# Packed attention with a gated FFN, one core: the first batch's loads, TensorE's first products and the first f tiles in another order

## The chip, the cores and the metric

One core of one Trainium2 chip runs the whole program. The metric is the device time of one execution in microseconds (us). The kernel before takes 739.77 us (median of 3 runs, 739.72 to 740.54).

## The reference

For each of 8 batches and 8 heads, 32 packed queries p attend over 576 keys and values, and the 576 queries q then attend over the 32 packed results. The output x, one row per token, goes through a gated feed-forward layer.

```python
def sm_attn(qq, kk, vv):                     # scale = 1 / sqrt(64)
    s = scale * np.matmul(qq, kk.transpose(0, 1, 3, 2))
    ...                                      # softmax a of s over the last axis
    return np.matmul(a, vv)
p_packed = sm_attn(p, k, v)                  # p: 8 x 8 x 32 x 64; q, k, v: 8 x 8 x 576 x 64
out = sm_attn(q, p_packed, p_packed)
x = out.transpose(0, 2, 1, 3).reshape(4608, 512)
return (x @ w_a) * (x @ w_b) @ w_out         # w_a, w_b: 512 x 1536; w_out: 1536 x 512
```

## The kernel before, in words

The work runs batch by batch; all of it is one stream on TensorE, with the other engines feeding it. For a batch:

- **Stage 1** (`stage1`, L241 on): scores of p against k (products at L247), softmax (maximum L253, exponential L257, both over two groups of heads e = 0, 1), its transposition (L271, L272) and the product with v (L281). The result pp is turned into `ppT` (L236, L237).
- **Stage 2** (`stage2`, L289 on): scores of q against pp (L297), a 32 x 32 transposition on VectorE (L302), maximum (L304), subtraction (L307), exponential (L309), sum and reciprocal (L312 to L314), multiplication (L315), transposition back (L318). The weights of the softmax are split in a high part `a_hi` (L319, ScalarE) and a low part `a_lo` (L86, VectorE) for TensorE's faster number format.
- **g tiles** (`g_tiles`, L324 on): the product of pp with the columns of w_a and w_b for a pair of f tiles (L332, 64x512 moving), split the same way into `ghi` (L338) and `glo` (L86). Since x = a2 @ pp, x @ w is computed as a2 @ (pp @ w).
- **First layer** (`mm1`, L355 on): for each of the 12 f tiles, 12 products of `ghi`, `glo` with `a_hi`, `a_lo` for the w_a half and 12 for the w_b half (L351); ScalarE copies one half (L363), VectorE multiplies (L366), the product is split into h_hi (L370) and h_lo (L86 on GpSimd).
- **Second layer** (`mm2_part`, L377): h times w_out into the output tiles.

The weights are read once, in pieces of 512 KB (`load_w`, `load_wout`), each as two 32-bit halves of what is stored. A piece takes three steps: A, `high_word` on ScalarE (L189); B, `low_word` on ScalarE, VectorE or GpSimd, as a digit of the string `WAYS` says (0: L197, 1 and 2: L194); C, `both_words` on VectorE (L200), which writes the piece into `w_ab`. A pool of 12 buffers holds pieces between load and C. Four pieces fill one pair of f tiles (index c).

The order on every engine is written out by hand. `FIRST` is the order of the first loads, `START` of everything up to the first product of `mm1`, `PLAN_0` and `PLAN` of what is put between the steps of `mm1` and `mm2` (slot by slot), as tokens: `T0` turns p, `k0` to `k4` and `q0` to `q4` turn pieces of k and q (`turn_first`, L147, L152, copies L149, L154, on the engine that the string `TURN` says), `S` and `r` step stage 1, `s` steps stage 2, `P0` turns pp, A, B, C convert a weight piece, `g` is the first pair of g tiles, and `W` puts nine products into TensorE's stream (`warm`, L524) whose result nobody reads. All loads of the first batch are issued from one queue, SyncE's (SP). A queue waits before a load until the load eight places before it, in the order in which the program issues them, has landed.

Of the kernel before, what the change touches and what calls it, by code (L numbers as in the profile page):

```python
# [9 lines left out]
F32R = mybir.dt.float32r  # L10
# [9 lines left out]
def tile_packed_attn_gated_ffn(  # L20
# [105 lines left out]
    def load_first(src, key, part):  # L126

        if part < 2:
            t = scratch.tile([P, R, 4 * D], F32, name=f"{key}n{part}")
            nc.sync.dma_start(  # L130
                out=t, in_=src[0, R * part:R * part + R, 0:4 * P, :].rearrange("h (p i) d -> p h (i d)", i=4))
        else:
            t = scratch.tile([P, H, 2 * D], F32, name=f"{key}n{part}")
            nc.sync.dma_start(out=t[0:TR], in_=src[0, :, 4 * P:S, :].rearrange("h (p u) d -> p h (u d)", u=2))
        firsts[key, part] = t
# [22 lines left out]
    def load_v(b, e):  # L158
# [5 lines left out]
        for i in range(4 // n):  # L164
            nc.sync.dma_start(
                out=t[:, :, n * i:n * i + n, :].rearrange("p r u d -> p r (u d)"),
                in_=vv[n * P * i:n * P * i + n * P].rearrange("(p u) r d -> p r u d", u=n).rearrange("p r u d -> p r (u d)"))
        for u in range(2):
            nc.sync.dma_start(
                out=t[TR * u:TR * u + TR, :, 4, :],  # L170
                in_=vv[4 * P:S].rearrange("(p u) r d -> u p r d", u=2)[u])
        vts[b, e] = t

    def load_p(b):
        t = sm.tile([P, E + 1, D], F32, name="p_nat", bufs=1)
        for e in range(E + 1):
            nc.sync.dma_start(out=t[:, e, :], in_=p[b].rearrange("(r e) j d -> e r j d", e=E)[e % E])  # L177
        p_nat[b] = t
# [27 lines left out]
    def load_w(c, n):  # L206

        w, rr = (w_a, w_b)[n // 2], n % 2
# [211 lines left out]
    def emit(b, plan, tasks={}):  # L420

        for name in plan.split():
# [3 lines left out]
            if name == "W":  # L426
                warm()
                continue
# [27 lines left out]
            elif what == "Lp":  # L456
# [4 lines left out]
    FIRST = ("p0 k0 k2 k1 q0 v0 q1 v1 q2 w1 w1 w1 w1 w1 w1 w1 w1 w1 w1 w1")  # L461
    START = ("T0 k0 k4 k1 k3 k2 q0 S0 S1 r0 r1 q1 r1 r0 r0 r1 r0 q2 r1 q3 q4 P0 s0 B s1 W A s0 B A A s0 s0 B s1 C "
             "A s1 B s0 C s1 A s1 C B B Lp2 C A B A s0 s1 B C B B s0 B g A C A A s1 Lv2 Lk2 C C A A C B B Lk3 C s1")
    WAYS = ("000000022220202120012012011200010010")
    TURN = ("0001110101")
    SUBS = ("0100")
# [4 lines left out]
    PLAN_0 = ("A | C C | B A B A | B C C B C | A A | C | B | C B A T0 k0 Lp2 A | A A B B C Lq0 | C C k1 | A B A | "  # L471
# [18 lines left out]
    def convert(x):  # L490
# [16 lines left out]
        else:  # L507
            assert len(to_do["A"]) <= len(to_do[x]) and len(to_do["B"]) <= len(to_do[x])
            if c < NC:
# [23 lines left out]
    for name in FIRST.split():  # L533
        what, i = name[0], int(name[1])
        if what == "p":
            load_p(0)
        elif what == "v":
            load_v(0, i)
        elif what == "w":
            load_pieces(i)  # L540
        else:
            load_first(k if what == "k" else q, what, i)
    gnext = []
    tasks = {"g": next_g(0)}
    emit(0, START, tasks)
    drain(tasks["g"])
    early.__exit__(None, None, None)
# [5 lines left out]
    for b in range(B):  # L553
        plan = dict(PLAN if b else PLAN_0)
        slot, tasks = [0], {"g": next_g(b + 1)}
# [5 lines left out]
        for ft in range(NFT):  # L561
            if ft % 2 == 0:
                gcur = list(gnext)
            elif ft + 1 < NFT:
# [64 lines left out]
```

## Time and profile before

| | |
|---|---|
| median of 3 runs | 739.77 us |
| the profiled execution, its own time | 739.7 us |
| its span (first to last instruction) | 737.9 us |
| outside the span | 1.8 us |
| TensorE busy | 724.8 us, 98% of the span |
| VectorE, ScalarE, GpSimd busy | 302.4, 282.6 and 212.5 us |
| data moved | 58.3 MB |

Times in the trace are microseconds from the span's start. TensorE has two records for one product, its weight load (PEld) and the product (PE); a product of two 4-byte operands is two instructions on it. "Idle before" is what an engine waited ahead of a row, with the instruction or load that ended the wait. The row of the granted clock in the page stands at full speed throughout; at which of its two levels TensorE ran is seen in the length of equal instructions.

### The profile page before, as it was taken

The numbers are of one execution on the slowest core, as the hardware profiler recorded it, in microseconds if no ns is written. First come the engines' busy times: TensorE is split into PE (matmuls) and PEld (weight loads), VectorE is DVE, ScalarE is ACT, GpSimd is POOL, SyncE is SP. The second block draws the span as 40 slices with busy tenths as digits, with TensorE's granted clock in tenths as the row PEclk, the third lists the DMA queues.
The fourth block names the chain that finished last, engine by engine and source line by source line (L and its number), as shares of the span: only waits on it lengthen the run. The fifth ranks groups of instructions, "written<-read, shape, count | busy, mean of one in ns | idle before, by whom it ended". The sixth has DMA issues, their size and how long they took to land.

```text
span 737.9 us, 13756 instructions
## 1 busy us (share of the span) xinstructions
PE 724.8 (98%) x5862; PEld 606.0 (82%) x5862; DVE 302.4 (41%) x487; ACT 282.6 (38%) x495; POOL 212.5 (29%) x154
## 2 busy tenths in 40 slices
PE   6899999999999999999999999999999999999998
PEld 4488977888888888888888888888888888888887
DVE  2888655456114561344503545045610456023200
ACT  3788744553125531444204442144311543134300
POOL 0586752334003340234202341033400334023300
PEclk9999999999999999999999999999999999999999
DMA  8999945250501514033310333115050100000001
GB/s 251 379 260 297 257 88 99 57 97 17 97 30 33 98 30 84 16 66 70 74 48 16 65 71 77 47 33 97 5 104 30 34 1 17 28 15 2 1 29 43
DMA packets 171005, 58.30 MB, mean 79 GB/s; under 512 B 140608, under 2 KB 158784, under 8 KB 170944
## 3 DMA queue, kind: packets, MB, share of 16 engines
q1 hardware_dynamic: 170944, 57.43, 31.9%
q8 instruction: 46, 0.75, 0.4%
q14 instruction: 15, 0.12, 0.1%
HBM read 47.97 MB, written 9.44 MB: 78 GB/s over the span
## 4 chain that ended last, share of the span: by engine, by line
PE 95%; DVE 2%; DMA 1%; ACT 1%; issue 0%; SPq 0%; DVEq 0%; ACTq 0%
PE m L351 42%; PE m L377 40%; PE x L332 6%; PE s L281 2%; PE s L247 1%; PE s L271 1%; PE s L297 1%; DMA raw<-in_moe_w_b_dram 1%; DMA kn<-in_k_dram 1%; PE x L236 0%; DVE w_ab L200 0%; PE x L147 0%; PE m L297 0%; PE m L147 0%; SPq L177 0%
## 5 line engine op out<-in xcount | busy, mean ns | idle before, releaser
L377 PE MATMUL m<-wo,h_hi 128*128 128x512 f32 (+1 forms) x888 | 268.7, 385 | 0.0
L86 POOL TENSOR_TENSOR h_lo<-asb,h_hi 128x576 fp32r<-128x576 f32 x96 | 139.1, 1449 | 411.5 <-ACT h_hi L370 411.2
L377 PEld LDWEIGHTS m<-wo,h_hi 128*128 128x128 f32 x888 | 164.2, 188 | 39.0 <-DVE t L302 5.0
L366 DVE TENSOR_TENSOR asb<-m,asb 128x576 f32<-128x576 f32 x96 | 72.7, 757 | 281.9 <-PE m L351 278.6
L351 PE MATMUL m<-a_hi,ghi 128*128 128x288 f32 x768 | 170.7, 304 | 1.6 <-ACT ghi L338 1.5
L377 PE MATMUL m<-wo,h_lo 128*128 128x512 f32 (+1 forms) x444 | 170.4, 384 | 0.0
L351 PE MATMUL m<-a_lo,ghi 128*128 128x288 f32 x768 | 164.0, 295 | 0.3 <-DVE a_lo L86 0.3
L351 PEld LDWEIGHTS m<-a_hi,ghi 128*128 128x128 f32 x768 | 122.2, 188 | 37.5 <-issue 15.9
L351 PE MATMUL m<-a_hi,glo 128*128 128x288 f32 x768 | 133.5, 295 | 0.0
L351 PEld LDWEIGHTS m<-a_lo,ghi 128*128 128x128 f32 x768 | 123.5, 188 | 0.5 <-DVE a_lo L86 0.5
L370 ACT CAST h_hi<-asb 128x576 fp32r<-128x576 f32 x96 | 64.7, 674 | 143.6 <-DVE asb L366 143.5
L351 PEld LDWEIGHTS m<-a_hi,glo 128*128 128x128 f32 x768 | 112.8, 188 | 0.2 <-DVE glo L86 0.2
L377 PEld LDWEIGHTS m<-wo,h_lo 128*128 128x128 f32 x444 | 83.4, 188 | 16.6
L86 DVE TENSOR_TENSOR glo<-x,ghi 128x512 fp32r<-128x512 f32 x96 | 61.8, 686 | 53.3 <-ACT ghi L338 53.3
L363 ACT COPY asb<-m 128x576 f32<-128x576 f32 x96 | 61.6, 641 | 36.7 <-PE m L351 29.0
L412 ACT COPY asb<-m 128x512 f32<-128x512 f32 x24 | 14.1, 587 | 134.8 <-PE m L377 133.6
L332 PE MATMUL x<-w_ab,ppT 64*32 64x512 f32 x768 | 55.4, 597 | 0.2 <-DVE w_ab L200 0.2
L338 ACT CAST ghi<-x 128x512 fp32r<-128x512 f32 x96 | 51.4, 588 | 5.9 <-PE x L332 5.9
L119 DVE STREAM_TRANSPOSE xT<-nat 128x1152 f32<-128x1152 f32 x28 | 38.3, 1368 | 0.0
L412 ACT COPY wo_f<-m 128x512 f32<-128x512 f32 x11 | 6.5, 588 | 55.2 <-PE m L377 55.2
L315 POOL TENSOR_TENSOR t<-t,sum 128x576 f32<-128x576 f32 x14 | 16.5, 1178 | 25.0 <-DVE sum L314 25.0
L189 ACT ACTIVATE raw<-raw 128x512 f32<-128x512 f32 x36 | 23.1, 683 | 0.1
(108 smaller groups left out, 408.1 us busy)
## 6 DMA issues: line engine op xcount, KB each, us to landing
nat<-in_k_dram SPq DMA_DIRECT2D x56, 144.0 KB
nat<-in_q_dram SPq DMA_DIRECT2D x56, 144.0 KB
vt<-in_v_dram SPq DMA_DIRECT2D x28, 256.0 KB
raw<-in_moe_w_a_dram SPq DMA_DIRECT2D x12, 512.0 KB
raw<-in_moe_w_b_dram SPq DMA_DIRECT2D x12, 512.0 KB
raw<-in_moe_w_out_dram SPq DMA_DIRECT2D x12, 512.0 KB
out_dram<-asb SPq DMA_DIRECT2D x17, 256.0 KB
out_dram<-wo_f SPq DMA_DIRECT2D x10, 256.0 KB
```

The costliest lines, as they stand in the source:

```text
L86: return eng.tensor_tensor(out=dst, in0=src, in1=hi.bitcast(F32), op=ALU.subtract)
L119: nc.vector.transpose(out=xT.rearrange("p h t -> p (h t)"), in_=t.rearrange("p h x d -> p (h x d)"))
L189: nc.scalar.activation(out=high, in_=high, func=AF.Prelu, scale=2.0 ** -112, alpha=-2.0 ** 32)
L315: eng.tensor_tensor(out=s2, in0=s2, in1=sum2.unsqueeze(2).broadcast_to([P, TU, J]), op=ALU.mult)
L332: nc.tensor.matmul(out=gps[e][J * r:J * r + J, :], lhsT=ppT[rows, 2 * (b % 2), r, :], rhs=w_ab[rows, c, r, :], start=True, stop=True)
L338: nc.scalar.copy(out=ghi[:, e], in_=gps[e])
L351: nc.tensor.matmul(out=ps[:, half, 0:HS], lhsT=gt[:, kt, i, :], rhs=at[:, kt, HS * half:HS * half + HS], start=(n == 0 and kt == 0), stop= ...
L363: nc.scalar.copy(out=asb, in_=pa[:, :, 0:HS])
L366: nc.vector.tensor_tensor(out=asb, in0=pb[:, :, 0:HS], in1=asb, op=ALU.mult)
L370: nc.scalar.copy(out=hh, in_=flat)
L377: nc.tensor.matmul(out=o[:, cols], lhsT=ht[:, c0:c0 + P], rhs=wt[:, cols], start=(ft == 0 and n == 0), stop=(ft == NFT - 1 and n == 2))
L412: nc.scalar.copy(out=ob, in_=o)
```

## The change

What it does:

- The loads of the first batch: k comes first, on SP's queue, then the first q tiles and the second v tile; p, the first v tile and the last piece of q are issued from ScalarE's queue (a capital letter in `FIRST`).
- `V13`: thirteen products of the 128x128 identity with itself stand at the head of TensorE's order, ahead of k; `W` becomes `W12`, twelve products instead of nine. Neither result is read.
- The first pair of f tiles is split: its weight pieces hold one f tile of w_a or w_b each, and `first_g` computes the g tiles of one f tile at a time, from two pieces (tokens `g` and `h`), with eight products of 256 columns for each.
- `TURN` moves four of the ten copies of turned k and q between VectorE and ScalarE, `SUBS` gives both subtractions and multiplications of stage 2 to GpSimd, `WAYS` moves the low words of some pieces, and `START` and `PLAN_0` are rewritten.

```diff
-    FIRST = ("p0 k0 k2 k1 q0 v0 q1 v1 q2 w1 w1 w1 w1 w1 w1 w1 w1 w1 w1 w1")
...
-    WAYS = ("000000022220202120012012011200010010")
-    TURN = ("0001110101")
-    SUBS = ("0100")
+    FIRST = ("k0 k1 k2 q0 P0 q1 V0 v1 w1 w1 w1 w1 w1 Q2 w1 w1 w1 w1 w1 w1")
+    START = ("V13 k1 T0 k3 k4 k0 k2 q0 S0 S1 r0 r1 q1 r1 r0 r0 r1 r0 B q2 r1 q3 A q4 P0 B C s0 s1 A A B W12 B s0 "
...
+    WAYS = ("100002012202202020012012011200010010")
+    TURN = ("1001000101")
+    SUBS = ("0000")
...
     def load_w(c, n):
+        if c == 0:
+            raw = wop.tile([P, R, P, 2], U32, name="raw", tag="w")
+            nc.sync.dma_start(
+                out=raw.rearrange("p r f t -> p r (f t)"),
+                in_=(w_a, w_b)[n % 2].bitcast(U32)[:, 2 * P * (n // 2):2 * P * (n // 2) + 2 * P].rearrange(
+                    "(r p) f -> p r f", p=P))
+            raws[c, n] = raw
+            return
...
-    def warm(n=9):
-        x = bank_pair()[:, 0, :]
-        t = firsts["k", 0].rearrange("p h t -> p (h t)")
+    def warm(t, n):
+        x = bank_pair()[:, 0, 0:t.shape[1]]
         for _ in range(n):
-            nc.tensor.matmul(out=x, lhsT=ident, rhs=t[:, 0:512], start=True, stop=True)
+            nc.tensor.matmul(out=x, lhsT=ident, rhs=t, start=True, stop=True)
+
+    def first_g(u, tiles):
...
+        gps = [bank() for _ in range(E)]
+        for r in range(R):
+            for e in range(E):
+                rows = slice(64 * e, 64 * e + 64)
+                nc.tensor.matmul(
+                    out=gps[e][J * r:J * r + J, 0:2 * P], lhsT=ppT[rows, 0, r, :],
+                    rhs=w_ab[rows, 0, r, :].rearrange("p (a u f) -> p u a f", a=2, u=2)[:, u],
+                    start=True, stop=True)
...
+        for e in range(E):
+            src = gps[e][:, 0:2 * P].rearrange("p (a f) -> p a f", a=2)
+            nc.scalar.copy(out=hi[:, e], in_=src)
+            lo_part(lo[:, e], src, hi[:, e])
...
+    tasks = {"g": first_g(0, firsts_g), "h": first_g(1, firsts_g)}
```

TensorE's order from its first instruction to the first scores of stage 1 (kn0, kn1, kn2 and qn0 are loaded pieces of k and q, p_nat is p). Before:

```order
L236 MATMUL x<-ident,p_nat 128x128 x2
L147 MATMUL x<-ident,kn_101 128x128 x4
L152 MATMUL x<-ident,kn_103 128x32 x8
L147 MATMUL x<-ident,kn_101 128x128 x4
L147 MATMUL m<-ident,kn_105 128x128 x8
L147 MATMUL x<-ident,qn_107 128x128 x4
L247 MATMUL s<-xT_147,pT 32x288 x2
```

And with the change:

```order
L535 MATMUL m<-ident 128x128 x13
L147 MATMUL x<-ident,kn_97 128x128 x4
L244 MATMUL x<-ident,p_nat 128x128 x2
L147 MATMUL m<-ident,kn_99 128x128 x4
L152 MATMUL x<-ident,kn_101 128x32 x8
L147 MATMUL x<-ident,kn_97 128x128 x4
L147 MATMUL m<-ident,kn_99 128x128 x4
L147 MATMUL x<-ident,qn_103 128x128 x4
L255 MATMUL s<-xT_157,pT 32x288 x2
```

The thirteen products stand in front, p behind the first piece of k, and the second half of k (kn_99) is wanted before the small last piece (kn_101).

TensorE's order from the second group of stage 2's scores to the first products of `mm1`. Before, and then with the change:

```order
L297 MATMUL m<-xT_185,ppT 32x288 x4
L524 MATMUL m<-kn_101,ident 128x512 x9
L332 MATMUL x<-w_ab,ppT 32x512 x8
L351 MATMUL m<-a_hi,ghi 128x288 x2
```

```order
L305 MATMUL m<-xT_199,ppT 32x288 x4
L535 MATMUL m<-kn_97,ident 128x512 x12
L544 MATMUL x<-w_ab,ppT 32x256 x16
L359 MATMUL m<-a_hi,ghi 128x288 x2
```

Twelve products instead of nine stand between the scores and the g tiles, and the g tiles of both f tiles (eight products each, sixteen in the row) still stand ahead of the first product of `mm1`.

The head of the two load queues. Before, all on SP's:

```order
L177 DMA p_nat<-in_p_dram 128x1x64 x3
L130 DMA kn_101<-in_k_dram 128x4x256
L134 DMA kn_103<-in_k_dram 32x8x128
L130 DMA kn_105<-in_k_dram 128x4x256
L130 DMA qn_107<-in_q_dram 128x4x256
L165 DMA vt<-in_v_dram 128x4x256
L169 DMA vt<-in_v_dram 32x4x64 x2
L130 DMA qn_113<-in_q_dram 128x4x256
```

With the change, SP's and then ScalarE's:

```order
L130 DMA kn_97<-in_k_dram 128x4x256
L130 DMA kn_99<-in_k_dram 128x4x256
L134 DMA kn_101<-in_k_dram 32x8x128
L130 DMA qn_103<-in_q_dram 128x4x256
L130 DMA qn_109<-in_q_dram 128x4x256
```

```order
L177 DMA p_nat<-in_p_dram 128x1x64 x3
L165 DMA vt<-in_v_dram 128x4x256
L169 DMA vt<-in_v_dram 32x4x64 x2
L134 DMA qn_129<-in_q_dram 32x8x128
L149 ACT_TABLE_LOAD
L149 COPY xT_158<-m 128x2x256
L149 COPY xT_157<-x 128x2x256
```

k goes to the head of SP's queue; p, the first v tile and the end of q are issued by ScalarE ahead of its first own instruction.

## Rows read from the trace of the kernel before

**Rows 1.** The page: TensorE's line of the busy times, and of the 40 slices of the span TensorE's busy tenths and the DMA engines'.

```profile
PE 724.8 (98%) x5862; PEld 606.0 (82%) x5862; DVE 302.4 (41%) x487; ACT 282.6 (38%) x495; POOL 212.5 (29%) x154
...
PE   6899999999999999999999999999999999999998
...
DMA  8999945250501514033310333115050100000001
```

**Rows 2.** What TensorE waited for in the whole span: engine, its line, what released it: us in total, times, longest.

```profile
PE x L236 <- DMA p_nat<-in_p_dram: 4.2, 1, 4.2
PE x L147 <- DMA kn<-in_k_dram: 2.2, 1, 2.2
PE m L351 <- ACT ghi L338: 1.5, 1, 1.5
...
PE m L351 <- DVE a_lo L86: 0.3, 1, 0.3
```

**Rows 3.** TensorE's timeline from 23 to 41 us, single rows of it.

```profile
23.90 7.99 PE L524 MATMUL m<-kn,ident 128*128 128x512 f32 x18
32.04 1.57 PE L332 MATMUL x<-w_ab,ppT 64*32 64x512 f32 x16 [0.15 <-DVE w_ab L200]
35.09 0.54 PE L351 MATMUL m<-a_hi,ghi 128*128 128x288 f32 x2 [1.48 <-ACT ghi L338]
...
37.68 0.53 PE L351 MATMUL m<-a_lo,ghi 128*128 128x288 f32 x2 [0.27 <-DVE a_lo L86]
...
39.20 1.22 PE L332 MATMUL x<-w_ab,ppT 64*32 64x512 f32 x16
```

**Rows 4.** The timeline of SP's queue from 0 to 19 us, in order of time: start, length of the issue (not of the transfer), what is loaded.

```profile
0.74 1.96 SPq L177 DMA_DIRECT2D p_nat<-in_p_dram  x3
2.74 0.48 SPq L130 DMA_DIRECT2D kn<-in_k_dram  x1
...
12.32 0.38 SPq L210 DMA_DIRECT2D raw<-in_moe_w_a_dram  x1
...
18.29 0.89 SPq L210 DMA_DIRECT2D raw<-in_moe_w_a_dram  x1
```

**Rows 5.** The DMA engines from 0 to 25 us, in 40 slices of 0.625 us: busy tenths, and GB/s moved.

```profile
DMA  0000227799999999999999999999999999999999
GB/s 0 0 0 23 46 47 98 184 349 370 271 295 341 351 354 347 352 332 276 295 342 351 353 304 215 239 305 390 387 383 393 380 390 397 374 383 393 387 374 400
```

**Rows 6.** TensorE's timeline from 7 to 21 us: start, length, what it does.

```profile
7.29 1.11 PE L147 MATMUL x<-ident,kn 128*128 128x128 f32 x4 [2.17 <-DMA kn<-in_k_dram]
8.33 1.06 PE L152 MATMUL x<-ident,kn 32*128 32x32 f32 x8
...
10.23 1.91 PE L147 MATMUL m<-ident,kn 128*128 128x128 f32 x8
11.93 1.06 PE L147 MATMUL x<-ident,qn 128*128 128x128 f32 x4
12.92 1.00 PE L247 MATMUL s<-xT,pT 64*32 64x288 f32 x24
13.74 0.90 PE L247 MATMUL m<-xT,pT 64*32 64x288 f32 x24
...
18.42 0.66 PE L147 MATMUL m<-ident,qn 128*128 128x128 f32 x4
...
20.43 0.68 PE L152 MATMUL x<-ident,qn 32*128 32x32 f32 x8
```

**Rows 7.** Timeline of VectorE, ScalarE and GpSimd from 24 to 36 us, single rows of the way from the scores of stage 2 to `a_hi` and `ghi`.

```profile
24.55 1.16 POOL L307 TENSOR_TENSOR s<-s,mx 128x576 f32<-128x576 f32 x1 [23.25 <-DVE mx L304]
...
25.74 0.69 ACT L309 ACTIVATE s<-s 128x576 f32<-128x576 f32 x1 [1.26 <-POOL s L307]
25.86 0.69 DVE L200 SCALAR_TENSOR_TENSOR w_ab<-raw 128x512 uint32<-128x512 uint32 x1
...
27.14 0.73 DVE L312 TENSOR_REDUCE sum<-s 128x18 f32<-128x576 f32 x1
...
28.54 1.41 POOL L315 TENSOR_TENSOR s<-s,sum 128x576 f32<-128x576 f32 x1 [2.83 <-DVE sum L314]
...
30.31 0.98 DVE L315 TENSOR_TENSOR s<-s,sum 128x576 f32<-128x576 f32 x1
...
32.42 1.43 DVE L318 STREAM_TRANSPOSE a2f<-s 128x576 f32<-128x576 f32 x2
33.22 1.33 ACT L319 CAST a_hi<-a2f 128x576 fp32r<-128x576 f32 x2 [1.15 <-DVE a2f L318]
```

**Rows 8.** Timeline of VectorE and the others from 1 to 22 us (ScalarE's table load, GpSimd's last step on the identity, a copy of turned k, the first maximum, pp, ppT).

```profile
0.73 1.28 ACT L154 ACT_TABLE_LOAD   x1 [0.73 <-PEq L613]
...
1.01 0.29 POOL masks.py:199 TENSOR_SCALAR_AFFINE_SELECT ident<-ident 128x128 f32<-128x128 f32 x1
...
12.18 0.69 DVE L149 COPY xT<-m 128x512 f32<-128x512 f32 x1 [1.01 <-PE m L147]
...
14.12 0.76 DVE L253 TENSOR_REDUCE nmx<-s 128x1 f32<-128x576 f32 x1 [1.25 <-PE s L247]
...
18.56 0.48 DVE L287 TENSOR_SCALAR pp<-x,rs 128x64 f32<-128x64 f32 x2 [1.08 <-PE x L281]
```

**Rows 9.** What SP's queue waited for between 17.3 and 18.8 us.

```profile
SPq L210 <- DMA raw<-in_moe_w_a_dram: 0.4, 1, 0.4
```

More of the change, by code (lines that the diff above doesn't have):

```diff
@@ L164, in load_v @@
         for i in range(4 // n):
-            nc.sync.dma_start(
+            eng.dma_start(
                 out=t[:, :, n * i:n * i + n, :].rearrange("p r u d -> p r (u d)"),
@@ L168, in load_v @@
         for u in range(2):
-            nc.sync.dma_start(
+            eng.dma_start(
                 out=t[TR * u:TR * u + TR, :, 4, :],
@@ L425, in emit @@
                 continue
-            if name == "W":
-                warm()
+            if name[0] in "VW":
+                warm(ident if name[0] == "V" else firsts["k", 0].rearrange("p h t -> p (h t)")[:, 0:512], int(name[1:]))
                 continue
@@ L508, in convert @@
             assert len(to_do["A"]) <= len(to_do[x]) and len(to_do["B"]) <= len(to_do[x])
-            if c < NC:
+            if c == 0:
+                col = 2 * P * (n % 2) + P * (n // 2)
+                both_words(w_ab[:, c, :, col:col + P], raw)
+            elif c < NC:
                 i, rr = divmod(n, 2)
@@ L517, in convert @@
             load_pieces(2)
-    def warm(n=9):
-        x = bank_pair()[:, 0, :]
-        t = firsts["k", 0].rearrange("p h t -> p (h t)")
+    def warm(t, n):
+        x = bank_pair()[:, 0, 0:t.shape[1]]
         for _ in range(n):
-            nc.tensor.matmul(out=x, lhsT=ident, rhs=t[:, 0:512], start=True, stop=True)
+            nc.tensor.matmul(out=x, lhsT=ident, rhs=t, start=True, stop=True)
+    def first_g(u, tiles):
+        assert len(to_do["C"]) <= len(pieces) - 2 * (u + 1)
+        gps = [bank() for _ in range(E)]
[6 more added lines that the diff above has]
+                    start=True, stop=True)
+        if u == 0:
+            tiles.extend(ld.tile([P, E, 4 * P], F32R, name=n, bufs=2) for n in ("ghi", "glo"))
+        hi, lo = (t.rearrange("p e (a u f) -> p u e a f", a=2, u=2)[:, u] for t in tiles)
+        for e in range(E):
+            src = gps[e][:, 0:2 * P].rearrange("p (a f) -> p a f", a=2)
+            nc.scalar.copy(out=hi[:, e], in_=src)
+            lo_part(lo[:, e], src, hi[:, e])
+        gnext.append((hi, lo))
+        yield
     def next_g(b):
@@ L533, in tile_packed_attn_gated_ffn @@
     for name in FIRST.split():
-        what, i = name[0], int(name[1])
+        what, i = name[0].lower(), int(name[1])
+        eng = nc.scalar if name[0].isupper() else nc.sync
         if what == "p":
-            load_p(0)
+            load_p(0, eng)
         elif what == "v":
-            load_v(0, i)
+            load_v(0, i, eng)
         elif what == "w":
@@ L541, in tile_packed_attn_gated_ffn @@
         else:
-            load_first(k if what == "k" else q, what, i)
+            load_first(k if what == "k" else q, what, i, eng)
     gnext = []
-    tasks = {"g": next_g(0)}
+    firsts_g = []
+    tasks = {"g": first_g(0, firsts_g), "h": first_g(1, firsts_g)}
     emit(0, START, tasks)
     drain(tasks["g"])
+    second_g = tasks["h"]
     early.__exit__(None, None, None)
@@ L554, in tile_packed_attn_gated_ffn @@
         plan = dict(PLAN if b else PLAN_0)
-        slot, tasks = [0], {"g": next_g(b + 1)}
+        slot, tasks = [0], {"g": next_g(b + 1), "h": second_g}
         def between():
@@ L561, in tile_packed_attn_gated_ffn @@
         for ft in range(NFT):
-            if ft % 2 == 0:
+            if b == 0 and ft == 1:
+                drain(second_g)
+            if ft % 2 == 0 or b == 0 and ft == 1:
                 gcur = list(gnext)
-            elif ft + 1 < NFT:
+            if ft % 2 and ft + 1 < NFT:
                 gnext[:] = g_tiles(b, ft // 2 + 1)
```

18 lines of the change are left out of this document (9 added, 9 removed), and 6 rows, old and new, of the table PLAN_0.

## The prediction

> **What bounds the kernel now.** I read the page first: TensorE is busy 98% of the span, and below that only in its first and its last slices [rows 1]. Then its waits over the whole span: nothing of note after the first product of the first layer, and before it mainly two loads (p 4.2 us, k 2.2 us) and one wait for ghi (1.5 us) [rows 2]. So TensorE's stream is the bound from the first g tiles on; what the change can give or cost is the time at which that stream starts, and how densely it runs just after. I take as marker the start of the g tiles of the second pair, 39.20 us [rows 3], from which TensorE runs on without a wait. What holds the start is read in four more views. SP's queue: three issues for p come first, so that k is issued only at 2.74 [rows 4]. The DMA engines: hardly any bytes before 4.4 us, then busy throughout [rows 5]. TensorE's timeline: from 7.29 to 12.9 it transposes without a pause, four in 1.06 to 1.11 and eight in 1.91, while four later ones take 0.66 [rows 6]; less a tail of 0.2, which the next ones cover, that is 0.85 against 0.45 for four. These are the engine's two levels, 1.2 and 2.4 GHz; the granted-clock column stands at full speed and does not tell them apart, the rows do. The clock rises near 13.7, where the scores (L247) get shorter. Last, the way from stage 2's scores to ghi, most of it VectorE's [rows 7].
>
> **Loads.** k's first issue moves from 2.74 to 0.74 [rows 4], so I read the curve of bytes 2.0 us earlier. Up to k's first tile 96 + 512 KB are issued, and it is there at 7.29, when 990 KB have moved [rows 5, 6]: later loads move beside it, and a load lands some 380 KB, or 1.1 us at 335 GB/s (mean of the slices from 5.0 to 10 us [rows 5]), after its own bytes are due. ScalarE issues p (1.96 us, as SP did), then the first v tile at 2.7; its bytes flow from 3.9 (k's did 1.1 us after its issue). By then 0.5 MB have moved, 0.4 of them k's. From here two queues share engines that are already full. No row shows two queues. The bounds: the engines take turns between the queues, or they serve what was issued first. Turns: v takes half until 3.9 + 1.02/0.335 = 6.95, then the end of v and of q (192 KB) half again; the second half of k is due at 7.55, its last piece at 8.2, the first q tile at 9.7. They land at 8.7, 9.3 and 10.8. In order of issue: 6.9, 7.2 and 8.8. I take turns, since the bytes of [rows 5] already show later loads moving beside earlier ones.
>
> The Trainium skill, DMA: Bandwidth & Descriptors, section Queues, rings and completion order, says that each DMA engine goes round robin between the queues that have work for it, packet by packet. By it the time is the one of turns, 738.6 below; a strict order of issue would give 737.8. No run here has shown it yet.
>
> **V13.** The identity is ready at 1.30 [rows 8]. A product of 4-byte operands is two instructions, 0.444 us each for 512 columns at the high level (18 in 7.99 [rows 3]); 128 columns take a quarter of that, and twice as much at the low level: 0.22, so 26 take 5.8 us, 1.4 to 7.2. If the clock rises on the way, it ends earlier, at best near 5.9. It delays the first k transpositions (landing 5.6) by at most 1.6 us, and they and p are through by 8.3: covered, since the second half of k lands at 8.7. What it brings is the high level for what follows: 6.4 us of nearly continuous work brought it before [rows 6], which is 7.8 here.
>
> **Transpositions and first scores.** From 8.7, at the high level: four of k (0.45), the eight small ones (from 9.35, 0.6: 0.68 in [rows 6] with its tail), four and four (0.45 each): done at 10.8. VectorE's copies of k and of q follow (0.69 each, overlapping by little [rows 8]), the scores beside them, and the first maximum starts at 12.3. By q alone (10.8, four transpositions, scores) it is 12.1. Before: 14.12 [rows 8]. **Gain so far 1.8 us.** ScalarE's own start: issues to about 5.3, table load 1.28 [rows 8], ready at 6.6, first wanted at 9.2. It is covered by 2.5 us.
>
> **To the end of stage 2's scores.** The same chain at the same clock, 23.90 - 14.12 = 9.78 us, so 22.1. Put into it: the low word of the first weight piece on VectorE between two steps of pp. It waits for the load. Before, the first piece was issued at 12.32 and landed at 18.2 [rows 4, 9], 5.9 later; now it is issued when the first q tile lands, 10.9, so it lands at 16.8; pp's first step is through at 19.04 - 1.8 = 17.2 [rows 8]. Covered, by 0.4.
>
> **Subtractions and multiplications on GpSimd.** Counted from the scores' end X (22.1): subtractions to X + 3.2 (1.16 each [rows 7]), exponentials to X + 3.95 (0.69), the first sum and its reciprocal to X + 3.75, no longer kept back by a weight piece and a subtraction on VectorE (0.7 before: 26.43 to 27.14 [rows 7]). Multiplications (1.41 each) end at X + 5.25 and X + 7.15, both a2f transposed at X + 7.95, a_hi at X + 8.6; then VectorE does a low word, a_lo and the fourth weight piece, to X + 9.65. Before, a_hi was through 10.6 after the scores [rows 7].
>
> **W12.** Twelve products of 0.888 take 10.65 us, three more than before: +2.66. They end at X + 10.65 = 32.7, a microsecond behind the last of the above. So the three are on the path, and the earlier a_hi and fourth piece are hidden behind them. Before, W was followed by the wait for a_hi and ghi, 35.09 - 31.89 = 3.2 us [rows 3]; now ghi needs only the g tiles. Eight products of 256 columns take half of a 1.0 us set, the other eight as much again, and ScalarE's two narrow copies run beside the second set: first product of the first layer at 32.7 + 1.25 = 34.0. Twice eight instead of eight wide ones: the same columns, no cost.
>
> **First f tile.** Before, 35.09 to 39.20, 4.1 us, with a gap ahead of a_lo [rows 3]. Now VectorE has to do glo, two weight pieces and the second a_lo after the g tiles, about 2.8 us from 33.9, and TensorE wants that a_lo 2.0 us after its start: a stall of 0.6, in place of 0.3; the narrower glo is there sooner and gives some of it back. I keep 4.1: second pair at 38.1 instead of 39.20. The split of the pieces itself moves the same bytes; it lets two pieces do for g, which stays unused as long as W12 and both sets stand ahead of the first layer. Later weight pieces are loaded 2 us earlier and buffers come free earlier (the first C at about 20 instead of 25.86 [rows 7]), so supply keeps its distance.
>
> **Sum.** 12.3 + 9.78 + 10.65 + 1.25 + 4.1 = 38.1, against 39.2: 1.1 us less. The profiled execution took 739.7 (0.07 under the median of the runs), so **738.6 us**. A measurement here tells about 0.2%, 1.5 us, from no change: the gain lies within that.
>
> **Rivals.**
> 1. *Order of issue*, or two queues moving more bytes. For it: rates of 390 GB/s occur later with equally busy engines [rows 5]. Against it: the row on bytes above. Then k is whole at 6.9 and V13 holds: transpositions from 8.1 to 10.0, maximum at 11.5, 737.8; with a clock that rises inside V13, 10.5 and 736.8.
> 2. *Slower: the low level lasts.* If V13 doesn't raise the clock, or the wait for k lowers it again, the sixteen transpositions from 8.7 take 3.55 and q 0.85, scores 1.1 [rows 6]: maximum at 14.3, later than before, and W12's surplus (0.75 against the old way to ghi) comes on top: 740.6. It decides from a maximum at 13.4. Against it: the clock held through pauses of a microsecond after 14 us before.
> 3. *Slower: the first q tile late.* The time is 739.7 + (q's landing - 12.1): at 239 GB/s (a slice near 15 us [rows 5]) q lands at 13.2, 740.8. For it: v and the end of q are in front of it. Against it: that rate lasted two slices.
> 4. *The change does less than it says*: W12 covers all, and new waits in the first f tiles (ScalarE has six conversions queued ahead of a copy that frees a buffer) cost up to 0.7: 739.3.
>
> **How the numbers follow.** Forecast 0.42, order of issue 0.30, low level 0.09, late q 0.11, waits later 0.08. Under 738.2 lie all of rival 1 and a quarter of the forecast's case, 0.41; over 741.2 a third of the slower ones and a rest for unseen stalls, 0.10; between, 0.49. The range reaches from rival 1 with the early clock to rival 3: 736.7 to 740.9.
>
> **What would show it.** Right: the second half of k turned from 8.7, first maximum at 12.3, the unread twelve from 22.1 to 32.7 with a_hi ready before their end, first layer at 34.0, second pair at 38.1. Wrong: four transpositions of k still at 0.85 after 8.5 us; VectorE waiting for the first piece ahead of pp; a maximum before 11.6; or a wait of TensorE after 40 us.

## The result: slower by half a per cent, and the profile after

The changed kernel takes 743.93 us (median, 742.63 to 744.30) where the kernel before takes 739.90 on the same chip: ratio 1.0051, 95% interval 1.0038 to 1.0064, or 4.0 us more. The forecast was 738.6, with a range up to 740.9. The profiled execution took 743.65 us, its span is 741.9.

First the page of after: TensorE's line, and of the 40 slices TensorE's busy tenths.

```profile
PE 730.6 (98%) x5910; PEld 611.6 (82%) x5910; DVE 303.2 (41%) x490; ACT 281.2 (38%) x494; POOL 213.8 (29%) x156
...
PE   7999999999999999999999999999999999999998
```

As in [rows 1], only the first and the last slice are not full. A slice is 18.5 us long, too coarse to place 4 us; TensorE's waits over the whole span place them at the head (engine, line, what released it: us in total, times, longest):

```profile
PE x L244 <- DMA p_nat<-in_p_dram: 3.8, 2, 3.0
...
PE x L544 <- DVE glo L86: 1.0, 1, 1.0
PE x L340 <- DVE glo L86: 0.9, 1, 0.9
...
```

Of the three waits of [rows 2], the one for k is gone and the one for ghi is gone, but p is still waited for, and two waits for a low part of the g tiles are new. TensorE's timeline, single rows (start, length, line, what it does, wait ahead of it):

```profile
1.36 4.59 PE L535 MATMUL m<-ident 128*128 128x128 f32 x26 [1.36 <-POOL ident masks.py:199]
5.79 0.60 PE L147 MATMUL x<-ident,kn 128*128 128x128 f32 x4
9.42 0.30 PE L244 MATMUL x<-ident,p_nat 128*128 128x128 f32 x1 [3.03 <-DMA p_nat<-in_p_dram]
10.51 0.33 PE L244 MATMUL x<-ident,p_nat 128*128 128x128 f32 x1 [0.79 <-DMA p_nat<-in_p_dram]
10.68 0.60 PE L147 MATMUL m<-ident,kn 128*128 128x128 f32 x4
11.21 1.05 PE L152 MATMUL x<-ident,kn 32*128 32x32 f32 x8
12.20 1.11 PE L147 MATMUL x<-ident,kn 128*128 128x128 f32 x4
...
25.63 10.57 PE L535 MATMUL m<-kn,ident 128*128 128x512 f32 x24
36.12 0.66 PE L544 MATMUL x<-w_ab,ppT 64*32 64x256 f32 x16
37.76 0.99 PE L544 MATMUL x<-w_ab,ppT 64*32 64x256 f32 x16 [0.97 <-DVE glo L86]
38.68 0.53 PE L359 MATMUL m<-a_hi,ghi 128*128 128x288 f32 x2
...
43.02 1.42 PE L340 MATMUL x<-w_ab,ppT 64*32 64x512 f32 x16 [0.88 <-DVE glo L86]
```

The marker of the prediction, the start of the second pair of g tiles, is at 43.02 instead of 39.20 [rows 3]: 3.8 us of the 3.95 between the two profiled executions. Behind the marker both take the same (700.6 and 700.5). V13 did its part: k's first four transpositions behind it last 0.60, where before they lasted 1.11 [rows 6]. Then TensorE stands for 3.0 us, because p, second in its order, has not landed. The rows behind the pause first last 0.60, then 1.05 to 1.11 again. The granted clock shows the same; stretches of 2 us, columns: length, TensorE busy (instructions), granted clock, DMA share, GB/s:

```profile
10.00:12.00 2.00, 1.49 (x13) 0.80 1.10 335
12.00:14.00 2.00, 2.00 (x12) 0.50 0.97 215
14.00:16.00 2.00, 2.00 (x34) 0.50 0.49 119
16.00:18.00 2.00, 2.00 (x44) 0.50 1.02 341
```

From 12 to 18 us TensorE ran at the lower of its two levels, 1.2 GHz; from 18 to 20 the granted clock is 0.99. The first maximum on VectorE therefore starts at 16.33 instead of 14.12 [rows 8]:

```profile
16.33 0.76 DVE L261 TENSOR_REDUCE nmx<-s 128x1 f32<-128x576 f32 x1 [0.59 <-PE s L255]
```

The late p reaches further than TensorE. ScalarE's timeline (ACTq rows are its DMA issues):

```profile
0.74 2.34 ACTq L177 DMA_DIRECT2D p_nat<-in_p_dram  x3
...
5.26 4.36 ACTq L169 DMA_DIRECT2D vt<-in_v_dram  x2
10.49 0.32 ACTq L134 DMA_DIRECT2D qn<-in_q_dram  x1
10.84 1.28 ACT L149 ACT_TABLE_LOAD   x1 [10.84 <-DMA p_nat<-in_p_dram]
12.13 0.59 ACT L149 COPY xT<-m 128x512 f32<-128x512 f32 x1
```

The last load of ScalarE's queue, the end of q, must wait until the load eight places before it, p's third, has landed. All that ScalarE does itself is queued behind that issue: the table load starts at 10.84 instead of 0.73 [rows 8], its first copy of turned k at 12.13. SP's queue, in the same way, waits for the v tile on ScalarE's:

```profile
7.84 6.30 SPq L169 DMA_DIRECT2D vt<-in_v_dram  x2
14.18 0.43 SPq L210 DMA_DIRECT2D raw<-in_moe_w_a_dram  x1
```

So the first weight piece is issued at 14.18, later than before (12.32 [rows 4]) and than forecast (10.9). Why p is late shows when the packets are counted by queue (q1 is SP's, q10 ScalarE's: packets, MB, share of the engines), here from 4.5 to 5.5 us:

```profile
q1 hardware_dynamic: 362, 0.35, 110.1%
q10 hardware_dynamic: 3, 0.00, 0.3%
```

p was issued from 0.74 to 3.08, and in this microsecond its queue moved 3 packets beside 362 of k on SP's; from 5.5 to 6.5 it moved none. The three loads of p are 384 packets of 256 bytes, one for each row; its queue had moved 129 packets from 3.5 to 4.5, and went on only from 6.5. So it is not all of p that was held back: its first load was through by 5.26, where the small v load that waits for it is issued. The second and the third are the late ones; TensorE turned p at 9.42 and 10.51, when they had landed.

### The profile page after: what moved, and what is told of

It is laid out like the page before. It is cut to its first block, busy times and chain, and to the rows that moved or that the text cites. A ratio compares the mean times of both kernels' runs of the same rounds, so it can differ in the third digit from the quotient of the medians.

```text
span 741.9 us, 13860 instructions
## 1 busy us (share of the span) xinstructions
PE 730.6 (98%) x5910; PEld 611.6 (82%) x5910; DVE 303.2 (41%) x490; ACT 281.2 (38%) x494; POOL 213.8 (29%) x156
## 4 chain that ended last, share of the span: by engine, by line
PE 93%; DMA 3%; DVE 1%; ACT 1%; issue 0%; ACTq 0%; POOL 0%; DVEq 0%; POOLq 0%
PE m L385 40%; PE m L359 39%; PE x L340 6%; DMA p_nat<-in_p_dram 2%; PE s L289 2%; PE m L535 1%; PE s L255 1%; DMA raw<-in_moe_w_b_dram 1%; PE s L305 1%; PE s L279 1%; PE x L244 1%; PE m L305 0%; DMA raw<-in_moe_w_a_dram 0%; PE m L147 0%; DVE asb L374 0%
## 5 line engine op out<-in xcount | busy, mean ns | idle before, releaser
L385 PEld LDWEIGHTS m<-wo,h_lo 128*128 128x128 f32 x444 | 83.4, 188 | 16.6
L86 DVE TENSOR_TENSOR glo<-x,ghi 128x512 fp32r<-128x512 f32 (+1 forms) x98 | 62.0, 674 | 55.0 <-ACT ghi L346 53.6
```

The costliest lines, as they stand in the source:

```text
L86: return eng.tensor_tensor(out=dst, in0=src, in1=hi.bitcast(F32), op=ALU.subtract)
L385: nc.tensor.matmul(out=o[:, cols], lhsT=ht[:, c0:c0 + P], rhs=wt[:, cols], start=(ft == 0 and n == 0), stop=(ft == NFT - 1 and n == 2))
```

## The experiments

Each median stands against the kernel before on the same chip. Where a run is said to give back some of the changed kernel's 4.0 us, two such differences are compared.

**Which load is late, and does it come from the queue?**

`e1_p_sp`, p on SP's queue behind k's first half:

```diff
-    FIRST = ("k0 k1 k2 q0 P0 q1 V0 v1 ...
+    FIRST = ("k0 p0 k1 k2 q0 q1 V0 v1 ...
```

> The change with p issued on SP's queue, right behind the first half of k, instead of on ScalarE's; all else as changed. Theory A (the late landing of p on ScalarE's queue, 9.4 and 10.5 us, is what put the first maximum at 16.3 instead of 12.3: TensorE waits, falls to the low clock level, and ScalarE's own start stands behind the wait for p): p lands by 7, the second half of k by 9, the transpositions run at the high level, first maximum 12.0 to 13.2, and 3 to 4 us come off: 740.0 to 741.0. Rival B (the second v tile and the weight pieces, which wait on SP for loads of ScalarE's queue, hold the rest back, so that an earlier maximum is lost again before the first layer): maximum earlier, but the first layer by less than 1.5 us: 742.5 to 743.5.

Measured: 744.48 against 740.71, ratio 1.0051 [1.0036, 1.0066]. p was turned at 8.26, but the change of order moved a wait. What SP waited for, and then TensorE's row for k's second half:

```profile
SPq L130 <- DMA vt<-in_v_dram: 3.4, 1, 3.4
```

```profile
11.12 1.12 PE L147 MATMUL m<-ident,kn 128*128 128x128 f32 x4 [2.44 <-DMA kn<-in_k_dram]
```

A load of k that comes later on SP's queue now has the v tile of ScalarE's queue eight places ahead of it, and k is whole only at 11.1. Both expectations missed. The run tells nothing of p alone; it shows that the wait for the load eight places before ties the two queues together.

`e5_only_p_act`, only p left on ScalarE's queue:

```diff
-    FIRST = ("k0 k1 k2 q0 P0 q1 V0 v1 w1 w1 w1 w1 w1 Q2 ...
+    FIRST = ("k0 k1 k2 q0 P0 q1 v0 v1 w1 w1 w1 w1 w1 q2 ...
```

> The change with only p on ScalarE's queue; the first v tile and the last piece of q are issued on SP's queue at the same places of the program. Theory A1 (p is late since SP's larger loads, issued beside it, are served ahead of it): p still lands at 8 to 10.5, ScalarE starts its table load only 1 to 2 us earlier, first maximum 14.5 to 16.3: 742 to 744. Theory A2 (p is late since v follows it in its own queue and the engines are shared three ways): p lands by 6, first maximum 12.3 to 13.5: 740 to 741.

Measured: 747.22 against 740.71, ratio 1.0083 [1.0067, 1.0099], above the range of either theory. The table load is back at 3.11, but p is turned at 9.36 and 11.38, as late as in the changed kernel. So v beside it on its queue is not what holds p. Packets by queue from 7.5 to 8.5 us:

```profile
q1 hardware_dynamic: 319, 0.31, 103.6%
q10 hardware_dynamic: 57, 0.01, 7.1%
```

With nothing but p on its queue, p still gets 57 packets of 376. Theory A1 has p's landing right; the profiled execution then lost more than after did behind it (the marker is at 46.50), which was not followed up.

`f2_t0_late`, p turned behind k and q in TensorE's order:

```diff
-    START = ("V13 k1 T0 k3 k4 k0 k2 q0 S0 ...
+    START = ("V13 k1 k3 k4 k0 k2 q0 T0 S0 ...
```

> The change with the two transpositions of p moved in TensorE's order from behind the first piece of k to behind q, just ahead of the first scores; loads as changed, p on ScalarE's queue. Theory A (TensorE's order makes k wait for p, and the three idle microseconds lower the clock): the second half of k is turned from 7.4 as it lands, but ScalarE's copies still stand behind p's landing (10.5) and its table load, 12.1 and 12.7, so the first maximum comes at 13.5 to 14.5 instead of 16.3, 1.5 to 2.5 us off the total: 741.5 to 742.5. Theory B (ScalarE's late start alone sets it): 15.5 to 16.3, 743 to 744.

Measured: 743.54 against 739.95, ratio 1.0041 [1.0026, 1.0055]. k is whole and turned from 7.47, the first q tile from 10.46, all at the high level. Then:

```profile
13.35 0.69 PE L244 MATMUL x<-ident,p_nat 128*128 128x128 f32 x2 [2.26 <-ACT xT L149]
```

TensorE no longer waits for p, but for ScalarE's copies, which stand behind p's landing and the table load. The late p reaches the first scores by two ways, and taking away one leaves the other: theory B's case.

`f3_loads_sp`, all loads of the first batch on SP's queue, p first as before; all else as changed. So the queue and p's place in the order change together:

```diff
-    FIRST = ("k0 k1 k2 q0 P0 q1 V0 v1 w1 w1 w1 w1 w1 Q2 w1 ...
+    FIRST = ("p0 k0 k1 k2 q0 v0 q1 v1 q2 w1 w1 w1 w1 w1 w1 ...
```

> The change with its load part undone: p first, then k, q, v, all on SP's queue in nearly the order of before (the second half of k ahead of its small last piece, as TensorE wants it); thirteen products, split g tiles, W12 and the new order stay. Theory A (the loads are what was lost; W12 and the wait for banks take about 2 us of what the head gains): first maximum 11.8 to 12.8, W from 21.2 to 21.8, second pair of g tiles at 39.0 to 39.6 instead of 43.0: 739.5 to 740.5, no gain over before. Theory B (the loss is in the order of the other engines): 742 to 743.5.

Measured: 740.97 against 739.95, ratio 1.0014 [1.0001, 1.0028]: 3.0 of the 4.0 us are back. That is theory A's case, though 0.5 above its range. TensorE's timeline:

```profile
7.10 0.66 PE L147 MATMUL x<-ident,kn 128*128 128x128 f32 x4 [0.28 <-DMA kn<-in_k_dram]
7.59 0.38 PE L244 MATMUL x<-ident,p_nat 128*128 128x128 f32 x2
...
22.68 10.57 PE L535 MATMUL m<-kn,ident 128*128 128x512 f32 x24
...
40.08 1.42 PE L340 MATMUL x<-w_ab,ppT 64*32 64x512 f32 x16 [0.89 <-DVE glo L86]
```

p no longer waits, the transpositions stay at the high level, and the unread products start at 22.68, 1.2 earlier than before [rows 3]. The marker is still 0.9 later than before: W12 takes 2.6 more.

`g5_k_act`, the queues exchanged, k on ScalarE's and the rest on SP's, p first there:

```diff
-    FIRST = ("k0 k1 k2 q0 P0 q1 V0 v1 w1 w1 w1 w1 w1 Q2 w1 ...
+    FIRST = ("p0 K0 K1 K2 q0 v0 q1 v1 q2 w1 w1 w1 w1 w1 w1 ...
```

> The change with the two queues exchanged: the three loads of k are issued on ScalarE's queue, p and all else on SP's, p first. Theory A (beside each other, small loads of 256-byte rows wait behind large ones of another queue, whichever queue it is): k's first half lands at 5.5 to 6.5 and p only at 7 to 10, first maximum 14 to 16.5, 742 to 744. Theory B (it is ScalarE's queue that is served later): p lands at 4.2 as in the kernel before, k's first half at 7 to 8.5, first maximum 12.5 to 14, 740.5 to 742. Theory C (neither holds and p was late for what stood behind it): p 4.2, k 5.6, first maximum 11.8 to 12.5, 739.5 to 740.5.

Measured: 741.31 against 739.94, ratio 1.0019 [1.0009, 1.0029]. p, on SP's queue now and first in it, is turned at 8.28 (after a wait of 1.31) and 9.19. Packets from 4.5 to 5.5 us:

```profile
q10 hardware_dynamic: 379, 0.35, 105.7%
q1 hardware_dynamic: 35, 0.01, 3.7%
```

The packets are theory A's, with the names of the queues exchanged: not ScalarE's queue is slow, but p's loads are beside k's. The time is not theory A's: first maximum at 13.23 and 741.31 lie in theory B's ranges. The pauses were shorter, the rows behind them stayed at the high level (0.60 at 9.36), and ScalarE's table load started at 2.37, since it no longer stood behind a wait for p. So with two queues still, 2.7 of the 4.0 us are back: a second queue by itself is not what cost the 4.0, but how late p came by it and what stood behind p.

`h1_two_large`, as `f3_loads_sp` but k's second half on ScalarE's queue:

```diff
-    FIRST = ("k0 k1 k2 q0 P0 q1 V0 v1 w1 w1 w1 w1 w1 Q2 w1 ...
+    FIRST = ("p0 k0 K1 k2 q0 v0 q1 v1 q2 w1 w1 w1 w1 w1 w1 ...
```

> The changed kernel with all loads of the first batch on SP's queue, p first (as f3_loads_sp, 740.97), but the second half of k (512 KB, rows of 1 KB) on ScalarE's queue: two large loads on two queues at once, p's small rows on SP's. Theory A (a queue whose load has small rows falls behind a queue with large rows, and two queues with large rows share evenly): the second half of k, issued at 0.74, is whole by about 7, before the first half or within 0.5 us of it; p (SP) falls behind it while it moves, lands at 6 to 8; between 4.5 and 6.5 us each queue moves at least a third of the packets as soon as k's first half flows on SP; k whole at about 8, a microsecond sooner than in f3_loads_sp. Theory B (one queue is served nearly alone whatever its rows, the one that has the most work waiting): one of the two halves lands at least 1.5 us before the other, with under a tenth of the packets for the slower queue in some microsecond in which both have large rows under way. Time: with A the first maximum at 12 to 12.9 and 740 to 741.5, since f3_loads_sp's later waits stay; with B 740.5 to 743.

Measured: 742.68 against 740.28, ratio 1.0021 [1.0006, 1.0037]. It doesn't decide what it was made for: k's second half was through by 4.5, when SP's half of k only began to flow behind p, so the two hardly moved together. The trace of `e1_p_sp` has that case, k's first half on SP's queue and the v tile on ScalarE's: 201 and 153 packets from 3 to 4 us, 179 and 206 from 4 to 5, so two large loads did share. But in `h1_two_large` p, issued at 0.73, moved nothing while that half of k did. Packets by queue from 2.5 to 3.5 us, where SP's has no row:

```profile
q10 hardware_dynamic: 307, 0.31, 90.6%
```

In `f3_loads_sp`, with one queue, p moved 180 packets in that microsecond. So k's first half came later (turned at 8.38, not 7.10), TensorE paused for 2.3 us, and the clock was at 0.50 from 10 to 14.

**What W12 and the g tiles cost**

`e3_w9`, nine unread products:

```diff
-    ... A A B W12 B s0 "
+    ... A A B W9 B s0 "
```

> The change with W9 instead of W12 (nine unread products of 512 columns, as before the change). Theory A (W12 ends last ahead of the g tiles; a_hi and the fourth weight piece are there about 0.2 us before its end in the changed kernel's trace, ScalarE's last high word just before): W ends 2.66 us earlier, then ScalarE's queue (second a_hi, a high word, ghi) ends last, and the first layer starts 1.0 to 1.5 us earlier: 742.4 to 742.9. Rival B (the unread products keep the clock up and are hidden anyway): no change, 743.9. Rival C (all of the three products count): 741.3.

Measured: 742.82 against 740.71, ratio 1.0026 [1.0016, 1.0037]. In its profile p came in as late as in after, and the head was 0.7 longer than in after. TensorE's timeline:

```profile
26.34 7.99 PE L535 MATMUL m<-kn,ident 128*128 128x512 f32 x18
...
37.13 1.22 PE L544 MATMUL x<-w_ab,ppT 64*32 64x256 f32 x16 [2.21 <-DVE glo L86]
```

2.58 us less of unread products, but the second set of g tiles then waits 2.2 instead of 1.0; from the start of the unread products to the marker it is 16.6 instead of 17.4. Of the three products 0.8 us are on the path. ScalarE then runs without a pause up to the first set's ghi (36.27), VectorE up to its glo (36.66): the queues of both end last. The medians give a larger gain, 2.1 us over before where the changed kernel has 4.0; the profiled execution, 743.29, is one of the slower of the ten, so the 0.8 is shown for it alone.

`e4_h_late`, the second set of g tiles behind the start of the first layer:

```diff
-    ... "C A Lk3 h C B")
+    ... "C A Lk3 C B")
-    PLAN_0 = ("A | C B C | ...
+    PLAN_0 = ("h A | C B C | ...
```

> The change with the g tiles of the second f tile (token h) moved from ahead of the first layer to the middle of the first f tile's products. Theory A (the second set waits 1.0 us for the two banks that glo of the first set has to leave, and stands ahead of the first layer with its own 0.9 us): first layer 1.3 to 1.4 us earlier, its first f tile longer by 0.5 for the set, and the 0.9 us wait of the next g tiles for banks stays or grows by some tenths: 743.0 to 743.6. Rival B (VectorE's row of weight pieces and glo ends last either way): no change, 743.7 to 744.2.

Measured: 744.19 against 740.71, ratio 1.0050 [1.0035, 1.0065]. TensorE's waits:

```profile
PE x L340 <- DVE glo L86: 1.3, 1, 1.3
PE m L359 <- DVE a_lo L86: 1.0, 1, 1.0
...
PE m L359 <- ACT ghi L553: 0.5, 1, 0.5
```

One wait of 1.0 is gone and waits of 1.0, 0.5 and 0.4 more have come. The a_lo and the glo that end the waits of 1.0 and 1.3 stand on VectorE behind weight pieces without a pause between them; theory B was right.

`f4_loads_sp_w9_h`, the edits of `f3_loads_sp`, `e3_w9` and `e4_h_late` together:

```diff
+    FIRST = ("p0 k0 k1 k2 q0 v0 q1 v1 q2 w1 ...
+    ... W9 ...
+    PLAN_0 = ("h A | C B C | ...
```

> As the kernel with the loads back on SP's queue, and W9 for W12, and the g tiles of the second f tile in the middle of the first f tile's products. Theory A: first layer from ScalarE's ghi, 10.7 us behind the scores of stage 2, 32.0 to 32.6; second pair of g tiles 36.8 to 37.8: 737.3 to 738.5, 1.5 to 2.5 us under the kernel before. Theory B (the weight pieces or VectorE then end last and give it back within the first f tiles): 739.3 to 740.3.

Measured: 742.16 against 739.95, ratio 1.0023 [1.0008, 1.0038]. In the profiled execution k's small last piece was 1.2 late and the clock low from 13 to 16, so that the marker stood at 40.93; the times of both theories were missed, and what the two edits bring together can't be read from it.

`g6_loads_sp_w9`, `f3_loads_sp` with nine products:

```diff
+    FIRST = ("p0 k0 k1 k2 q0 v0 q1 v1 q2 w1 ...
+    ... W9 ...
```

> The change with its loads back on SP's queue (741.0 where the kernel before took 739.9) and W9 for W12. Theory A (of the three products 0.8 us are on the path, since ScalarE's ghi and the two banks end next): second pair of g tiles 16.6 behind the start of W instead of 17.4; 739.8 to 740.5. Theory B (what follows is bound by loads and conversions): no change, 740.7 to 741.5.

Measured: 741.83 against 739.94, ratio 1.0023 [1.0014, 1.0032], 0.3 above theory B's range. The marker is at 39.20, as before, and yet the kernel is 1.9 slower. (The nine products took 9.26 us here instead of 7.99: the granted clock was 0.50 from 23 to 25, behind two waits of 0.6 each. So the marker doesn't price the three products.) The only wait of TensorE from 44 to 80 us, where before has none:

```profile
PE m L359 <- ACT asb L371: 1.9, 2, 1.4
```

Of it 0.5 ends at 48.7 and 1.4 at 58.05 (TensorE is busy for 6.60 of the 8 us from 50 to 58), and together they have the size of the whole difference. The copy at 57.37 that TensorE waits for stands on ScalarE behind a high word, and that waits for its weight piece:

```profile
56.81 0.65 ACT L189 ACTIVATE raw<-raw 128x512 f32<-128x512 f32 x1 [1.68 <-DMA raw<-in_moe_w_a_dram]
```

So the stream runs into loads that come late, through ScalarE's queue, as theory B had it.

**What an earlier start is worth by itself**

`f1_v13_before`, the kernel before with the thirteen products in front and nothing else:

```diff
-    START = ("T0 k0 k4 k1 ...
+    START = ("V T0 k0 k4 k1 ...
```

> The kernel before with one part of the change alone: thirteen unread products of the identity at the head of TensorE's order, then p, k and the rest as before, loads all on SP's queue. Theory A (with p and k landing one behind the other as before, the high clock level that the thirteen bring lasts through the transpositions): transpositions from 7.3 at 0.45 for four, bounded by the landing of k and q, first maximum 11.8 to 12.6 instead of 14.1, first layer earlier by 1 to 2 us: 737.9 to 739.2 where the kernel before takes 739.9. Theory B (the wait for k's first half, or transpositions themselves, let the clock fall again, as in the changed kernel): transpositions at 0.85, maximum at 14.1 or later: 739.7 to 740.5.

Measured: 743.02 (739.76 to 743.79) against 739.95, ratio 1.0025 [1.0009, 1.0042]. TensorE's timeline, then a wait of it, then two stretches with the granted clock:

```profile
7.20 0.66 PE L147 MATMUL x<-ident,kn 128*128 128x128 f32 x4 [1.05 <-DMA kn<-in_k_dram]
...
21.60 7.99 PE L528 MATMUL m<-kn,ident 128*128 128x512 f32 x18
...
37.80 1.20 PE L332 MATMUL x<-w_ab,ppT 64*32 64x512 f32 x16
```

```profile
PE s L247 <- DVE xT L119: 2.3, 1, 2.3
```

```profile
62.00:64.00 2.00, 2.00 (x12) 0.59 1.06 391
64.00:66.00 2.00, 2.00 (x11) 0.56 1.02 412
```

V13 alone does what it was costed for: the high level from 7.2, the first maximum at 12.27 as theory A had it, the unread products 2.3 earlier, the marker at 37.80, 1.4 earlier. But the time is in neither theory's range: TensorE then reaches the second batch's scores before that batch's k is there. k landed at 59.6, TensorE waited 2.3 us, and behind the pause it ran at the low level from 62 to 66. The ten runs fall into two groups (four from 739.8 to 741.1, six from 743.0 to 743.8); the profile is of the second, and that k comes in time in the first is inferred, not seen.

`g1_v13_v_late` also moves a v load of the second batch behind its k; `g2_v_late` is that move without V13:

```diff
-    ... A s1 Lv2 Lk2 C C A A C B B Lk3 C s1")
+    ... A s1 Lk2 C C A A C B B Lk3 Lv2 C s1")
```

> The kernel before with the thirteen unread products at the head, as in the run that had only those, and in addition the second batch's first v tile loaded behind the second half of its k instead of ahead of the first. Theory A (what the thirteen win at the head, 1.4 us at the second pair of g tiles, was lost again to a wait of 2.3 us for the second batch's k and to the low clock level after it): k's second half lands 2 to 3 us earlier, the wait is gone, 738.0 to 739.0. Theory B (the loads are one saturated stream, so something else comes late in its place, a weight piece or v): a wait elsewhere, 740 to 743.

> The kernel before with only that move of the v tile's load: the control. Theory A: no wait was there to take away, so no change, 739.5 to 740.3. Theory B (some executions of the kernel before do wait for that k, which spreads its times): the median stays within 0.5 us and the slower runs (741 and over) are fewer.

Measured: 740.08 with V13, ratio 1.0004 [0.9994, 1.0013], and 740.88 without, 1.0009 [1.0000, 1.0019]. k is in time now, the wait for it and the low level behind it are gone, and with them most of `f1_v13_before`'s loss. With V13 the marker is 0.7 earlier than before, but the time is not: theory B. The control came out 0.9 slower than before, more than either of its theories allowed; against it V13 is worth 0.8, within the spread of both. TensorE's wait in `g1_v13_v_late`, and what held ScalarE ahead of it:

```profile
PE m L351 <- ACT asb L363: 1.5, 2, 1.3
```

```profile
61.69 0.67 ACT L189 ACTIVATE raw<-raw 128x512 f32<-128x512 f32 x1 [3.95 <-DMA raw<-in_moe_w_a_dram]
```

The two waits lie between 58 and 74 us and take twice what the head had saved; the longer one ends at 64.85, and ScalarE had stood for 3.95 us for a weight piece before that. The next bound stands right behind the last, and no version beat the kernel before.

## Why the prediction was wrong

The terms of the sum, as forecast and as measured:

| term | forecast | after | difference |
|---|---|---|---|
| first maximum | 12.3 | 16.33 | +4.0 |
| to the end of stage 2's scores | 9.78 | 9.30 | -0.5 |
| W12 to the g tiles | 10.65 | 10.49 | -0.2 |
| to the first layer | 1.25 | 2.56 | +1.3 |
| to the second pair | 4.1 | 4.34 | +0.2 |
| marker | 38.1 | 43.02 | +4.9 |

- **Loads: the step that failed.** The prediction took even turns between two queues and priced the large loads by them; p, issued first on its own queue, got no price. One sentence of V13 puts the wait for it at nothing: k's first transpositions "and p are through by 8.3: covered". p was through at 10.8, and TensorE waited 3.8 us for it. The runs show what stands in its place: beside k on the other queue p's second and third load moved 3 packets of 365 in one microsecond and none in the next; the same shows with the queues exchanged (35 of 414) and, less strongly, with p alone on its queue (57 of 376); and with p ahead of k on one queue 3.0 of the 4.0 us are back. For k the turns were too pessimistic: its second half was turned at 7.47 in `f2_t0_late` (forecast 8.7; in order of issue it was due at 6.9), the first q tile at 10.46 (10.8). The Trainium skill, DMA: Bandwidth & Descriptors, section Queues, rings and completion order, has each engine go round robin between queues by packets, a packet there being several descriptors. A packet of the trace is one row (512 for a load of 512 KB in rows of 1 KB), so that rule by itself doesn't fix these counts. Even turns are seen from 7.5 to 8.5 us of after, where the queues moved 184 and 185 packets, with v on ScalarE's. From 4.5 to 6.5 they are not, and the measurement decides. Whether a queue without packets had descriptors ready then, no trace here shows.
- **ScalarE's own start, "covered by 2.5 us".** The prediction counted the length of ScalarE's issues, to 5.3, and not the wait ahead of the last of them. The price was a table load at 10.84, and the rule for it stands in the description of the kernel: eight places. It was applied to SP's queue and not to ScalarE's. `f2_t0_late` shows that it keeps the kernel slow where TensorE no longer waits for p itself (743.54), and `e5_only_p_act` that p's lateness does so without it (747.22).
- **Rival 2, the low level lasts, happened by another cause.** "If ... the wait for k lowers it again" was the clause; the wait was p's. Its price (maximum at 14.3) left out the pause itself, so that the 740.6 given was too little. The clock's turning back is shown by the granted clock and by 1.05 to 1.11 against 0.60 to 0.68. A pause of 2.1 to 2.3 us stands ahead of the low level in `h1_two_large`, `e5_only_p_act` and `f1_v13_before` also. But in `g5_k_act` pauses of 1.3 and 0.6 were followed by the high level, and in `g6_loads_sp_w9` two of 0.6 by the low one, so the length of a pause alone doesn't tell.
- **V13 was right.** The high level behind it, and the start of the unread products 2.3 earlier, are shown in `f1_v13_before`. It ended between 5.9 and 7.3 us, from run to run (7.2 forecast).
- **W12 was right in size and wrong in what hides behind it.** The g tiles start 2.35 later after the scores' end than before (forecast 2.66). Missed: the second set needs the two banks from which VectorE takes the first set's low part, and that comes 1.0 late; it makes up most of the +1.3 to the first layer. VectorE was not busy then, it waited for ScalarE's high part, which had waited 1.2 for the first set itself:

```profile
37.28 0.76 DVE L86 TENSOR_TENSOR glo<-x,ghi 128x256 fp32r<-128x256 f32 x2 [1.31 <-ACT ghi L553]
```

  So this wait is the way from product to high part to low part, which the term of 1.25 left out by letting ScalarE's copies run beside the second set. The 0.9 ahead of the next pair is VectorE's queue: there glo stands behind weight pieces without a pause. When three products are taken away, ScalarE's and VectorE's queues end last, and 0.8 comes back, not 2.6 (`e3_w9`). The second a_hi (34.43 to 35.1) and the fourth piece (to 35.96) did end before the unread products, as forecast.
- **"Supply keeps its distance" was wrong, though after never came to test it.** The whole forecast gain of 1.1 assumed that an earlier marker is an earlier end. `f1_v13_before`, `g6_loads_sp_w9` and `g1_v13_v_late` each moved the marker up or kept it and lost the gain, nearly all of it between 50 and 74 us. The profiled times less the marker say the same: 700.3 to 700.8 in the seven kernels of the changed order whose marker is at 42.3 or later, 701.4 to 702.4 in the four (`f3_loads_sp`, `f4_loads_sp_w9_h`, `g5_k_act`, `g6_loads_sp_w9`) with it at 40.9 or earlier. So even with p in time, 738.6 is not to be expected with this order of the second batch; no run reached the marker of 38.1 with it.
- **Two of its signs of being wrong came**: transpositions at the low level (1.05 to 1.11, from 11.21 on), and a wait of TensorE after 40 us (0.88, ahead of the marker).

Open: why p's packets are held back. The size of its rows, 256 bytes, is one candidate. Another, which no run isolates, is that loads of both queues are made into packets in the order of issue: in after, p's first load moved from 4.0 on, when k's first half, issued with it, was through, and the other two from 6.5 on, behind k's second half and last piece, which were issued ahead of them. Against it, 39 rows of q moved on p's own queue from 5.5 to 6.0 in `g5_k_act`, ahead of p's second load, which had been issued first. Open too are the split of `f1_v13_before`'s runs; and what of the last 1.0 us of `f3_loads_sp` is the head's (0.9 at the marker) and what the later wait for asb (0.7 in its profile), since its interval holds either.

## What to carry to other kernels

A second DMA queue was no faster lane here: before a small load goes there, ask what large loads run at that time, and which waiting issue would stand ahead of the issuing engine's own work. When a start is moved up, follow the supply of the next stage through its first use; here what was gained at the head was asked back at the second batch's k, or at weight pieces that ScalarE waited for ahead of its copies. And a pause of TensorE costs more than its length where the rows behind it run at the low level (four transpositions in 1.11 instead of 0.60).

## What the runs showed that was not expected

- Small loads beside large ones on another queue can nearly stand still: of p, 96 KB in rows of 256 bytes, issued from 0.74 to 3.08, a third was through by 5.3 and the rest only by 10.5. On one queue, ahead of k, it was turned at 7.6 without a wait.
- The waits for p, 3.0 and 0.8 us, were followed by 6 us at the granted clock of 0.50, from 12 to 18.
- Equal heads differ from one execution to the next: the thirteen products took 4.6 to 5.9 us over these profiles, and the head of `e3_w9` stands 0.7 us behind that of after, with p's second turn 0.3 later.
